# Two MLPs behind a delta attention: the second MLP's first weight blocks split during the first MLP, in single conversion steps, with raw blocks asked for later

## The chip, the core and the metric

The kernel runs on one core of a Trainium2 chip. The metric is device microseconds of one execution. Three timed runs of the kernel before gave 1169.36 us as the median (1157.91 to 1170.28).

## What is computed

```python
x = attention(q, k, v, beta)            # delta rule, 4 x 8 heads, 768 steps, head size 48
x = x.transpose(0, 2, 1, 3).reshape(3072, 384)

h = x @ w_in                            # first Mlp, d_ff = 2048
P = a[0] + a[1] * h + a[2] * h**2 + a[3] * h**3
Q = 1 + abs(b[0]) * abs(h) + abs(b[1]) * h**2
x = (P / (Q + 1e-6)) @ w_out

h = x @ w2_in                           # second Mlp, d_ff = 2048
out = (h * tanh(softplus(h))) @ w2_out  # Mish
```

All weights arrive in 64 bits. A conversion turns each pair of 32-bit words into one float32.

## The kernel before

The attention runs first, by a plan. Then come two Mlps in one software pipeline of 192 units, 96 for each: six groups g of 512 tokens, and in each group 16 blocks f of 128 hidden features. Unit i is one (g, f). In the loop over i each iteration emits, in the order of a string of `MLP_OPS`, steps of several units at once; `LAGS` says by how many units a step is behind.

Products are made of three passes: each float32 operand is split into a high part (rounded to the matmul's type) and a low part (the rest), and hi*hi, hi*lo and lo*hi are summed in PSUM. Unit i has an up-projection of nine matmuls (`up`, L827) into one of two PSUM banks h, and four units later a down-projection (`down`: L913 in the first Mlp, L946 in the second) into banks o. At the end of a group ACT evicts o through ev (L1035).

In the first Mlp the activation of a unit is spread over the engines: ACT takes q = |h| (L857); r = b1*q + b0 on ACT (L864, even units) or POOL (L860, odd units and units near an x split, by `m1.pool`); ACT s = a3*h + a2 (L866); POOL q = q*r (L870); ACT Ln (L877) and Exp (L879) for the quotient; VectorE the polynomial in two steps on h (L884, L886; behind L886 the bank h is free for the up-projection two units later) and three more (L893, L897, L902) that end in g. Two units later ACT makes the high part gh (L838) and POOL the low part (L842). In the order of ACT, Ln and Exp of unit i-1 come first in iteration i, then L857 of unit i, r, s, and gh of unit i-2. In the order of VectorE the three steps of unit i-1 come before the two of unit i.

The next group's x is split in units 11, 12 and 13 of each group: on ACT the high part (L807, ops "xa"), on VectorE the low one (L811, "xB").

The second Mlp's activation is two Mish instructions on ACT (L932 for the high part, L937 for g) and a subtraction for the low part (L842), on POOL where `m2.pool` has the unit and on VectorE elsewhere.

Weights. The first Mlp's 16 blocks are converted and split during the attention and stored in DRAM; two stay in SBUF, the other 14 are fetched at the start of the first Mlp (L730), all by SP's queue. The ring of tiles w holds 16 blocks. Block f of the second Mlp is needed from unit 96 + f.

The second Mlp's weights are converted by `Conv`, two sides (w_in, w_out) a block. A side is one raw load of 384 KB (L651), the magnitude (L663 on ACT, or L659 on VectorE once `free` is set) and three pulled steps on VectorE: "size" (L668, L672), "sign" (L678) and "low" (L684). When "low" of side j is emitted, the raw load of side j+3 is, too. What comes behind "low" is appended to a list of ACT work that op "f" empties at the end of the iteration. For the first eight blocks (`DIRECT`) that is a DMA from wm to DRAM, unsplit (L692); those blocks are fetched from iteration 94 on into wraw (L727), split by ACT (L733, op "wa") and by POOL (L737, op "wb") in iterations 95 to 102. For the other eight blocks, converted from unit 97 on at four steps an iteration, ACT copies the high part to w (L694) and POOL subtracts (L699).

In the first Mlp op "c" pulls three steps at once, in every fifth iteration: 12, 17, 22, ... 87. The first three raw loads are asked for by `conv.start()` ahead of the loop, before the first weight fetch.

Of the kernel before, what the change touches and what calls it, by code (L numbers as in the profile page):

```python
# [9 lines left out]
F32 = mybir.dt.float32  # L10
# [22 lines left out]
MLP_OPS = [  # L33
# [4 lines left out]
]  # L38
# [3 lines left out]
}  # L42
CONV_START, CONV_EARLY, CONV_RATE = 8, 16, 4

# [576 lines left out]
class Weights:  # L621
# [9 lines left out]

    def __init__(self, nc, w_in, w_out, sb, kept, direct, scratch):
        self.nc, self.sb, self.kept, self.direct, self.scratch = nc, sb, kept, direct, scratch
        self.w_in = w_in.rearrange("(k p) f -> p k f", p=128)
        self.w_out = w_out.rearrange("f (k c) -> f k c", c=128)
        self.raw = {}
        self.t = {}

    def tile(self, f):
        if f not in self.t:  # L640
            self.t[f] = self.sb.tile([128, 2, 2, 3, 128], F32R, "w")
        return self.t[f]

    def convert(self, f, side):
# [44 lines left out]
        def out():  # L689
            m = w["m"].bitcast(F32).rearrange("p (k c) -> p k c", k=3)  # L690
            if f not in self.direct:
                nc.sync.dma_start(out=self.scratch[f][:, side], in_=m)  # L692
                return
            nc.scalar.copy(out=self.tile(f)[:, 0, side], in_=m)  # L694
# [5 lines left out]

        return get, mag, size, sign, low, out, rest

    def plan(self, p, fs):

        slots = len(self.kept)
        for i, f in enumerate(fs):
            slot, late = f"w{i % slots}", LATE * i - AHEAD
            for side in range(2):
                n = 2 * i + side
                get, mag, size, sign, low, out, rest = self.convert(f, side)  # L710
                raw, m = f"w64{n % 2}", f"wm{n % 2}"
# [12 lines left out]

    def fetch(self, f):
        self.raw[f] = self.sb.tile([128, 2, 3, 128], F32, "wraw")
        self.nc.sync.dma_start(out=self.raw[f], in_=self.scratch[f])  # L727
# [4 lines left out]
    def hi(self, f):  # L732
        self.nc.scalar.copy(out=self.tile(f)[:, 0], in_=self.raw[f])  # L733

    def lo(self, f, engine="P"):
        t = self.tile(f)
        (self.nc.gpsimd if engine == "P" else self.nc.vector).tensor_tensor(  # L737
            out=t[:, 1], in0=self.raw.pop(f), in1=t[:, 0].bitcast(F32), op=ALU.subtract
        )


class Conv:


    def __init__(self, sides, direct):
        self.sides, self.direct = sides, direct
        self.act = []
        self.n = 0
        self.mags = 0
# [15 lines left out]
    def pull(self, n):  # L765
        for _ in range(n):
# [14 lines left out]
            if i == 2:  # L781
                self.act.append(side[5] if j < self.direct else lambda side=side: (side[5](), side[6]()))
                if j + 3 < len(self.sides):
                    self.sides[j + 3][0]()
# [172 lines left out]
def tile_delta_attention_two_mlps(  # L957
# [43 lines left out]

    wd = [[dram.tile([128] + [2] * (2 - n) + [3, 128], F32, name=f"w{n}_{f}") for f in range(NF)] for n in range(2)]
    w1 = Weights(nc, moe_w_in, moe_w_out, sb, range(FQ), range(NF), wd[0])
    w2 = Weights(nc, moe2_w_in, moe2_w_out, sb, (), range(DIRECT, NF), wd[1])
    def run(fns):
        for fn in fns:
            fn()

    conv = Conv([w2.convert(f, side) for f in range(NF) for side in range(2)], 2 * DIRECT)

# [66 lines left out]
    with ExitStack() as bctx:  # L1077
        sb2 = bctx.enter_context(tc.tile_pool(name="sb2", bufs=1, reuse_waits="tile"))
        ps2 = bctx.enter_context(tc.tile_pool(name="ps2", bufs=1, space=PSUM, reuse_waits="tile"))
        sb.add(sb2, w=16 - FQ, w64=1, wm=1, wraw=3, x=1, q=3, s=3, r=2, g=3, gh=5, ev=3)  # L1080
        ps.add(ps2, h=2, o=4, r=2)
        conv.start()
        fetch_w = {n: (w1.fetch_split, FQ + LOOK + n) for n in range(NF - FQ - LOOK)}
        split_w = {}
        for f in range(DIRECT):
            fetch_w[n1 - 2 + f] = (w2.fetch, f)
            split_w[n1 - 1 + f] = (w2, f)
        for f in range(LOOK):
# [10 lines left out]
        ups, downs = {}, {}  # L1099
        m1.pool = {i for i in range(n1) if i % 2 or i in split_w or any(starts(j) for j in range(i + 3, i + 6) if j < n2)}  # L1100
        m2.pool = [i for i in range(n1, n1 + NF) if i % 2]
        for i in range(n2 + max(LG.values())):
            kind = 3 if i >= n1 else 2 if i in split_w and i >= n1 - 1 else 0 if i in split_w else 1

# [6 lines left out]
            for op in LISTS[kind]:  # L1111
# [22 lines left out]
                elif op == "fx" and i + 8 < n2 and starts(i + 8):  # L1134
                    mlp(i + 8).fetch_x(units[i + 8][0])
                elif op == "wa" and i in split_w:
                    w, f = split_w[i]
                    w.hi(f)
                elif op in ("wb", "wB") and i in split_w:
                    w, f = split_w[i]  # L1140
                    w.lo(f, "P" if op == "wb" else "V")
# [41 lines left out]
```

## Time and profile before

| | us |
|---|---|
| median of three timed runs | 1169.36 |
| the profiled execution, its own time | 1159.04 |
| its span, first to last instruction | 1157.3 |
| TensorE busy | 1044.8 |
| VectorE busy | 722.6 |
| ACT busy | 612.6 |
| POOL busy | 532.6 |

The attention fills the span to about 320 us, the first Mlp goes on to about 735, the second to the end. Busy times are shares of engines that take turns; what limits a stage is read from what each engine waits for there. In a row of the trace, the number in brackets is the idle time of the engine in front of the instruction, and behind the arrow stands what ended it. "w" in a row is any of the weight tiles or raw tiles.

### The profile page before, as it was taken

How to read it: one execution, taken by the hardware profiler on the slowest of the kernel's cores; microseconds unless marked ns; L12 is line 12 of the kernel's file. 1: busy time of each engine (PE TensorE's matmuls, PEld its weight loads, DVE VectorE, ACT ScalarE, POOL GpSimd, SP SyncE). 2: the span in 40 equal slices, each digit the busy share in tenths (PEclk: the TensorE clock that was granted, in tenths of full speed). 3: DMA queues.
4: the chain of work that ended last, by engine and by line, in shares of the span. 5: the costliest groups of instructions: out<-in, count | busy, mean ns of one | idle time of the engine just before them, and what ended most of it. 6: DMA issues, size and time to landing. Idle time of an engine off the chain costs nothing.

```text
span 1157.3 us, 24281 instructions
## 1 busy us (share of the span) xinstructions
PE 1044.8 (90%) x9980; PEld 903.6 (78%) x9980; DVE 722.6 (62%) x1214; ACT 612.6 (53%) x1093; POOL 532.6 (46%) x607
## 2 busy tenths in 40 slices
PE   5649869688879898999999999999999999999998
PEld 4538868577858777877778778678999999999997
DVE  5877575995658999899898999786121121212110
ACT  4415445334468787888888888754333223333322
POOL 3178787477347676777677767774000000000000
PEclk9858879789889999999999999999999999999999
DMA  7427676226692020120212022152100001010000
GB/s 140 84 64 179 171 209 146 77 58 194 189 364 105 21 96 21 48 69 21 76 41 76 21 69 89 36 197 68 55 1 30 26 1 55 1 55 1 28 1 28
DMA packets 122415, 92.90 MB, mean 80 GB/s; under 512 B 79936, under 2 KB 106688, under 8 KB 122304
## 3 DMA queue, kind: packets, MB, share of 16 engines
q1 hardware_dynamic: 122048, 91.25, 26.9%
q8 instruction: 78, 1.28, 0.4%
q14 instruction: 33, 0.27, 0.1%
q0 software_dynamic: 256, 0.10, 0.1%
HBM read 63.02 MB, written 28.31 MB: 79 GB/s over the span
## 4 chain that ended last, share of the span: by engine, by line
PE 46%; POOL 17%; DVE 14%; ACT 12%; issue 9%; DMA 2%; SPq 0%; POOLq 0%; DVEq 0%; ACTq 0%
PE h L827 17%; PE o L946 15%; POOL q L870 8%; ACT r L877 3%; POOL r L860 3%; POOL gh L842 3%; PE y_ps L562 3%; ACT q L857 2%; PE c_ps L524 2%; ACT r L879 2%; PE c_ps L507 2%; PE s_all L547 2%; PE o L913 2%; DVE tmp L447 1%; PE t_ps L348 1%
## 5 line engine op out<-in xcount | busy, mean ns | idle before, releaser
L827 PE MATMUL h<-x,w 128*128 128x512 f32 x1728 | 435.8, 397 | 23.2 <-DVE s L886 12.1
L827 PEld LDWEIGHTS h<-x,w 128*128 128x128 f32 x1728 | 323.8, 190 | 97.6 <-DVE s L886 26.7
L842 DVE TENSOR_TENSOR gh<-g,gh 128x512 fp32r<-128x512 f32 x88 | 63.8, 725 | 285.3 <-ACT g L937 285.3
L946 PE MATMUL o<-w,gh 128*128 128x384 f32 x1152 | 217.4, 337 | 2.0 <-ACT ev L1035 2.0
L913 PE MATMUL o<-gh,w 128*128 128x512 f32 x864 | 213.7, 391 | 0.5 <-ACT ev L1035 0.4
L946 PEld LDWEIGHTS o<-w,gh 128*128 128x128 f32 x1152 | 204.5, 188 | 10.8 <-ACT ev L1035 2.7
L913 PEld LDWEIGHTS o<-gh,w 128*128 128x128 f32 x864 | 162.8, 189 | 36.2 <-ACT ev L1035 2.2
L932 ACT ACTIVATE gh<-h 128x512 fp32r<-128x512 f32 x96 | 57.6, 600 | 213.0 <-PE h L827 213.0
L870 POOL TENSOR_TENSOR q<-q,r 128x512 f32<-128x512 f32 x96 | 127.9, 1332 | 80.4 <-ACT r L864 75.9
L842 POOL TENSOR_TENSOR gh<-g,gh 128x512 fp32r<-128x512 f32 x104 | 136.8, 1315 | 8.9 <-ACT g L937 4.9
L877 ACT ACTIVATE r<-q,cst 128x512 f32<-128x512 f32 x96 | 66.4, 692 | 61.0 <-POOL q L870 60.8
L893 DVE SCALAR_TENSOR_TENSOR q<-q,r 128x512 f32<-128x512 f32 x96 | 65.6, 683 | 27.4 <-ACT r L879 27.0
L699 POOL TENSOR_TENSOR w<-wm,w 128x384 fp32r<-128x384 f32 x48 | 48.4, 1009 | 72.5 <-ACT w L694 71.9
L866 ACT ACTIVATE s<-h,ab 128x512 f32<-128x512 f32 x96 | 74.4, 775 | 0.0
L886 DVE SCALAR_TENSOR_TENSOR s<-s,ab,h 128x512 f32<-128x512 f32 x96 | 71.8, 748 | 3.4
L897 DVE SCALAR_TENSOR_TENSOR r<-s,ab,r 128x512 f32<-128x512 f32 x96 | 71.8, 748 | 0.0
L884 DVE TENSOR_TENSOR s<-s,h 128x512 f32<-128x512 f32 x96 | 65.4, 681 | 10.1 <-ACT s L866 10.1
L902 DVE SCALAR_TENSOR_TENSOR g<-q,r 128x512 f32<-128x512 f32 x96 | 65.9, 687 | 3.3
L453 POOL TENSOR_TENSOR xs<-xs,tmp 128x30 f32<-128x30 f32 (+14 forms) x120 | 62.2, 519 | 9.4
L857 ACT ACTIVATE q<-h 128x512 f32<-128x512 f32 x96 | 57.1, 595 | 12.6 <-PE h L827 12.6
L860 POOL TENSOR_SCALAR r<-q,ab 128x512 f32<-128x512 f32 x54 | 43.4, 804 | 43.1 <-ACT q L857 43.1
L447 POOL TENSOR_TENSOR tmp<-xs 128x30 f32<-128x30 f32 (+14 forms) x120 | 58.5, 487 | 7.0
(123 smaller groups left out, 1322.9 us busy)
## 6 DMA issues: line engine op xcount, KB each, us to landing
w<-w SPq DMA_DIRECT2D x28, 768.0 KB, 7.4
w<-in_moe_w_in_dram SPq DMA_DIRECT2D x32, 384.0 KB, 3.7
w<-in_moe_w_out_dram SPq DMA_DIRECT2D x32, 384.0 KB, 3.6
xraw<-x SPq DMA_DIRECT2D x36, 256.0 KB, 4.0
kn<-in_k_dram SPq DMA_DIRECT2D x48, 96.0 KB, 3.5
qn<-in_q_dram SPq DMA_DIRECT2D x48, 96.0 KB, 3.3
v<-in_v_dram SPq DMA_DIRECT2D x48, 96.0 KB, 3.4
x<-yst SPq DMA_DIRECT2D x24, 192.0 KB, 4.1
```

The costliest lines, as they stand in the source:

```text
L447: eng.tensor_tensor(out=tv, in0=ls[:, j, j + 1:HC].unsqueeze(1).to_broadcast([128, j, n]), in1=xs[:, 0:j, j:j + 1].to_broadcast([128, j, n ...
L827: self.nc.tensor.matmul(out=self.st[i]["h"], lhsT=self.w.t[f][:, a, 0, k], rhs=self.x[g][:, b, k], start=(n == 0), stop=(n == 8),)
L842: (nc.gpsimd if engine == "P" else nc.vector).tensor_tensor(out=s["gh"][:, 1], in0=s["g"], in1=s["gh"][:, 0].bitcast(F32), op=ALU.subtract)
L857: nc.scalar.activation(out=s["q"], in_=s["h"], func=ACTF.Abs)
L860: nc.gpsimd.tensor_scalar(out=s["r"], in0=s["q"], scalar1=k["b1"], scalar2=k["b0"], op0=ALU.mult, op1=ALU.add)
L866: nc.scalar.activation(out=s["s"], in_=s["h"], func=ACTF.Identity, scale=k["a3"], bias=k["a2"])
L870: nc.gpsimd.tensor_tensor(out=s["q"], in0=s["q"], in1=s["r"], op=ALU.mult)
L877: nc.scalar.activation(out=s["r"], in_=s["q"], func=ACTF.Ln, bias=k["c"])
L886: nc.vector.scalar_tensor_tensor(out=s["s"], in0=s["s"], scalar=k["a1"], in1=s["h"], op0=ALU.add, op1=ALU.mult)
L897: nc.vector.scalar_tensor_tensor(out=s["r"], in0=s["s"], scalar=k["a0"], in1=s["r"], op0=ALU.add, op1=ALU.mult)
L913: self.nc.tensor.matmul(out=self.acc[g][d], lhsT=self.w.t[f][:, a, 1, d], rhs=self.st[i]["gh"][:, b], start=(first and n == 0), stop=(last ...
L946: self.nc.tensor.matmul(out=self.acc[g][t][:, 0:384], lhsT=self.st[i]["gh"][:, a, t * 128:(t + 1) * 128], rhs=self.w.t[f][:, b, 1].rearran ...
```

## The change

- The first eight blocks of the second Mlp are treated as the others: ACT copies the high part (into a tile wt, of which there is one), POOL subtracts, and after the second side a DMA stores the split block (768 KB). They are fetched split, straight into w, in iterations 86 to 93. The fetch into wraw, L733 and L737 with the ops "wa" and "wb" are gone, and two of the four strings of `MLP_OPS` with them.
- In the first Mlp, op "c" works only in iterations of `calm`: 6 to 87 without those that split x (11, 12 and 13 of each group). The 48 steps of the 16 sides are spread over these 67 iterations, at most one in each. "Low" falls into iterations 10, 17, 21, 25, 32, 37, 41, 48, 52, 56, 64, 68, 72, 79, 83 and 87.
- `conv.start()` moves into iteration 3, behind eight weight fetches.
- `m2.pool` takes all of the second Mlp's first 16 units, no longer the odd ones alone.

```diff
-CONV_START, CONV_EARLY, CONV_RATE = 8, 16, 4
+CONV_START, CONV_RATE = 6, 4
...
+        self.tag = {f: "wt" for f in passing}
...
-            self.t[f] = self.sb.tile([128, 2, 2, 3, 128], F32R, "w")
+            self.t[f] = self.sb.tile([128, 2, 2, 3, 128], F32R, self.tag.get(f, "w"))
...
-            if f not in self.direct:
-                nc.sync.dma_start(out=self.scratch[f][:, side], in_=m)
-                return
             nc.scalar.copy(out=self.tile(f)[:, 0, side], in_=m)
...
+        def done():
+            if side and f in self.tag:
+                self.store(f)
...
     def store(self, f):
+        self.tag.pop(f, None)
...
-                self.act.append(side[5] if j < self.direct else lambda side=side: (side[5](), side[6]()))
+                self.act.append(lambda side=side: [f() for f in side[5:]])
...
-        conv.start()
...
-            fetch_w[n1 - 2 + f] = (w2.fetch, f)
-            split_w[n1 - 1 + f] = (w2, f)
+            fetch_w[n1 - NF + 6 + f] = (w2.fetch_split, f)
+        calm = [i for i in range(CONV_START, n1 - 8) if not any(starts(i + 5 - k) for k in range(3))]
...
-        m2.pool = [i for i in range(n1, n1 + NF) if i % 2]
+        m2.pool = range(n1, n1 + NF)
...
+            if i == CONV_START - 3:
+                conv.start()
...
-                elif op == "c" and i >= CONV_START:
-                    conv.pull(max(0, 3 * min(CONV_EARLY, CONV_EARLY * (i + 1 - CONV_START) // (n1 - 8 - CONV_START)) - conv.n))
+                elif op == "c" and i in calm:
+                    conv.pull(6 * DIRECT * (calm.index(i) + 1) // len(calm) - conv.n)
```

How the instructions stand on three engines. Line numbers of the change are lower: L682 is L684 of before, L689 is L694, L825 is L838, L864 is L877, L866 is L879, L873 is L886, L880 is L893.

SP's queue at the start of the first Mlp, behind the last stores of the attention. Before, three raw loads and then the first fetches:

```order
L651 DMA w_4760<-in_moe_w_in_dram 128x3x128
L651 DMA w_4762<-in_moe_w_out_dram 128x384
L651 DMA w_4764<-in_moe_w_in_dram 128x3x128
L730 DMA w<-w_2_82 128x1536
L730 DMA w<-w_3_83 128x1536
```

And with the change:

```order
L613 DMA x_5_65<-yst_155 48x8x128 x4
L726 DMA w<-w_2_82 128x1536
L726 DMA w<-w_3_83 128x1536
L726 DMA w<-w_4_84 128x1536
L726 DMA w<-w_5_85 128x1536
L726 DMA w<-w_6_86 128x1536
L726 DMA w<-w_7_87 128x1536
L726 DMA w<-w_8_88 128x1536
L726 DMA w<-w_9_89 128x1536
L649 DMA w_4850<-in_moe_w_in_dram 128x3x128
```

Eight fetches now stand ahead of the first raw load.

VectorE in iteration 12 of the kernel before, where a side is converted in one piece behind the low part of x (L811):

```order
L884 TENSOR_TENSOR s<-s,h 128x512
L886 SCALAR_TENSOR_TENSOR s<-s,ab,h 128x512
L811 TENSOR_TENSOR x<-xraw,x 128x512
L668 TENSOR_SCALAR wm<-wm 128x384
L672 TENSOR_SCALAR wm<-wm 128x384
L678 SCALAR_TENSOR_TENSOR wm<-w_4760,wm 128x384
L684 SCALAR_TENSOR_TENSOR wm<-w_4760,wm 128x384
L893 SCALAR_TENSOR_TENSOR q<-q,r 128x512
```

With the change, iteration 10 has "low" alone on VectorE:

```order
L871 TENSOR_TENSOR s<-s,h 128x512
L873 SCALAR_TENSOR_TENSOR s<-s,ab,h 128x512
L682 SCALAR_TENSOR_TENSOR wm<-w_4850,wm 128x384
L880 SCALAR_TENSOR_TENSOR q<-q,r 128x512
L884 SCALAR_TENSOR_TENSOR r<-s,ab,r 128x512
```

"Size" and "sign" of that side stand in iterations 7 and 8, between L873 and L880 as "low" does here.

ACT at the end of iteration 10 and the start of iteration 11, with the change (the kernel before has L838 and then L877 here, with nothing between them):

```order
L853 ACTIVATE s<-h,ab 128x512
L825 CAST gh<-g 128x512
L689 CAST wt<-wm 128x384
L864 ACTIVATE r<-q,cst 128x512
L866 ACTIVATE r<-r 128x512
L844 ACTIVATE q<-h 128x512
```

The copy to wt, which reads what "low" wrote, stands between gh of unit 8 and Ln (L864) of unit 10. There are 16 such places.

## Rows read from the trace of the kernel before

**Rows 1.** The page: the chain that ended last, shares of the span by line.

```profile
PE h L827 17%; PE o L946 15%; POOL q L870 8%; ACT r L877 3%; POOL r L860 3%; POOL gh L842 3%; PE y_ps L562 3%; ACT q L857 2%; PE c_ps L524 2%; ACT r L879 2%; PE c_ps L507 2%; PE s_all L547 2%; PE o L913 2%; DVE tmp L447 1%; PE t_ps L348 1%
```

**Rows 2.** Windows: stretch, us, each engine's busy us, granted clock, DMA share, GB/s.

```profile
330.00:340.00 10.00, 8.97 (x26) 6.90 (x27) 4.68 (x7) 5.29 (x10) 3.16 (x3) 0.68 1.02 420
...
338.20:735.30 397.10, 385.03 (x1656) 311.00 (x1657) 364.45 (x544) 329.50 (x553) 281.97 (x238) 0.99 0.19 64
...
735.30:763.00 27.70, 22.57 (x94) 16.75 (x94) 21.64 (x37) 17.14 (x30) 22.75 (x16) 1.00 0.36 117
```

**Rows 3.** Timeline of units 9 and 10: start, us, engine, line, operation.

```profile
363.38 0.59 ACT L857 ACTIVATE q<-h 128x512 f32<-128x512 f32 x1
...
366.34 0.69 ACT L877 ACTIVATE r<-q,cst 128x512 f32<-128x512 f32 x1 [1.19 <-POOL q L870]
...
367.56 0.59 ACT L857 ACTIVATE q<-h 128x512 f32<-128x512 f32 x1
...
370.34 1.29 POOL L842 TENSOR_TENSOR gh<-g,gh 128x512 fp32r<-128x512 f32 x1
370.41 0.69 ACT L877 ACTIVATE r<-q,cst 128x512 f32<-128x512 f32 x1 [0.23 <-POOL q L870]
370.46 0.75 DVE L886 SCALAR_TENSOR_TENSOR s<-s,ab,h 128x512 f32<-128x512 f32 x1
...
371.63 0.59 ACT L857 ACTIVATE q<-h 128x512 f32<-128x512 f32 x1
```

**Rows 4.** ACT from 338.20 to 735.30 by line (busy, mean ns, idle before), and its timeline.

```profile
L877 ACT ACTIVATE r<-q,cst 128x512 f32<-128x512 f32 x92 | 63.6, 692 | 56.0 <-POOL q L870 55.9
...
L857 ACT ACTIVATE q<-h 128x512 f32<-128x512 f32 x93 | 55.3, 595 | 6.3 <-PE h L827 6.3
...
342.78 0.59 ACT L857 ACTIVATE q<-h 128x512 f32<-128x512 f32 x1
...
407.79 0.59 ACT L857 ACTIVATE q<-h 128x512 f32<-128x512 f32 x1
...
412.44 0.61 ACT L857 ACTIVATE q<-h 128x512 f32<-128x512 f32 x1
...
735.10 0.60 ACT L857 ACTIVATE q<-h 128x512 f32<-128x512 f32 x1
```

**Rows 5.** VectorE by line in that stretch, then the timeline around unit 15.

```profile
L684 DVE SCALAR_TENSOR_TENSOR wm<-w,wm 128x384 int32<-128x384 int32 x16 | 15.1, 942 | 0.6
...
382.23 1.54 DVE L684 SCALAR_TENSOR_TENSOR wm<-w,wm 128x384 int32<-128x384 int32 x1
...
387.19 3.91 PE L827 MATMUL h<-x,w 128*128 128x512 f32 x9 [3.01 <-DVE s L886]
```

**Rows 6.** Timeline of the first Mlp's start; the last row: DMA issues there.

```profile
320.01 0.67 SPq L651 DMA_DIRECT2D w<-in_moe_w_in_dram  x1
...
330.32 7.17 PE L827 MATMUL h<-x,w 128*128 128x512 f32 x18 [6.41 <-DMA w<-w]
...
334.54 0.60 ACT L857 ACTIVATE q<-h 128x512 f32<-128x512 f32 x1 [4.42 <-PE h L827]
...
w<-in_moe_w_in_dram SPq DMA_DIRECT2D x2, 384.0 KB, 5.5
```

**Rows 7.** The hand-over, 735.3 to 763, by line.

```profile
L827 PE MATMUL h<-x,w 128*128 128x512 f32 x45 | 12.3, 406 | 3.1 <-ACT w L733 1.2 <-ACT g L937 1.1 <-POOL w L737 0.8
L737 POOL TENSOR_TENSOR w<-wraw,w 128x768 fp32r<-128x768 f32 x6 | 11.5, 1916 | 3.2 <-ACT w L733 3.2
...
L699 POOL TENSOR_TENSOR w<-wm,w 128x384 fp32r<-128x384 f32 x4 | 4.2, 1039 | 2.5 <-ACT w L694 2.5
...
L946 PE MATMUL o<-w,gh 128*128 128x384 f32 x12 | 2.8, 355 | 2.0 <-ACT ev L1035 2.0
...
L684 DVE SCALAR_TENSOR_TENSOR wm<-w,r 128x384 int32<-128x384 int32 x5 | 2.8, 551 | 0.1
L694 ACT CAST w<-wm 128x384 fp32r<-128x384 f32 x5 | 2.6, 521 | 7.9 <-DVE wm L684 7.9
```

More of the change, by code (lines that the diff above doesn't have):

```diff
@@ L33 @@
 MLP_OPS = [
[1 row of a table removed]
     "fx fw y0 1e 1f y1 u0 u1 u2 1a 1b 1c 1i 1j 1k 1d 1g 1h y2 d0 d1 d2 d3 xa 1L 1m xB c f",
[2 rows of a table removed]
+    "fx fw y0 1e 1f y1 2a 2b u0 u1 u2 1i 1j 1k y2 d0 v0 2M d1 v1 d2 v2 d3 v3 xa 1L 1m xB c f",
 ]
@@ L630, with __init__ @@
     word = None
-    def __init__(self, nc, w_in, w_out, sb, kept, direct, scratch):
-        self.nc, self.sb, self.kept, self.direct, self.scratch = nc, sb, kept, direct, scratch
+    def __init__(self, nc, w_in, w_out, sb, kept, passing, scratch):
+        self.nc, self.sb, self.kept, self.scratch = nc, sb, kept, scratch
+        self.tag = {f: "wt" for f in passing}
         self.w_in = w_in.rearrange("(k p) f -> p k f", p=128)
         self.w_out = w_out.rearrange("f (k c) -> f k c", c=128)
-        self.raw = {}
         self.t = {}
@@ L699, in rest @@
             nc.gpsimd.tensor_tensor(out=t[:, 1, side], in0=m, in1=t[:, 0, side].bitcast(F32), op=ALU.subtract)
-        return get, mag, size, sign, low, out, rest
+        def done():
+            if side and f in self.tag:
+                self.store(f)
+        return get, mag, size, sign, low, out, rest, done
     def plan(self, p, fs):
@@ L709, in plan @@
                 n = 2 * i + side
-                get, mag, size, sign, low, out, rest = self.convert(f, side)
+                get, mag, size, sign, low, out, rest, _ = self.convert(f, side)
                 raw, m = f"w64{n % 2}", f"wm{n % 2}"
@@ L722, in store, with __init__ @@
     def store(self, f):
+        self.tag.pop(f, None)
         self.nc.sync.dma_start(out=self.scratch[f], in_=self.t.pop(f).bitcast(F32))
-    def fetch(self, f):
-        self.raw[f] = self.sb.tile([128, 2, 3, 128], F32, "wraw")
-        self.nc.sync.dma_start(out=self.raw[f], in_=self.scratch[f])
     def fetch_split(self, f):
         self.nc.sync.dma_start(out=self.tile(f).bitcast(F32), in_=self.scratch[f])
[L732 to L739, printed above, removed]
 class Conv:
-    def __init__(self, sides, direct):
-        self.sides, self.direct = sides, direct
+    def __init__(self, sides):
+        self.sides = sides
         self.act = []
@@ L1000, in tile_delta_attention_two_mlps @@
     n2 = len(units)
-    wd = [[dram.tile([128] + [2] * (2 - n) + [3, 128], F32, name=f"w{n}_{f}") for f in range(NF)] for n in range(2)]
-    w1 = Weights(nc, moe_w_in, moe_w_out, sb, range(FQ), range(NF), wd[0])
-    w2 = Weights(nc, moe2_w_in, moe2_w_out, sb, (), range(DIRECT, NF), wd[1])
+    wd = [[dram.tile([128, 2, 2, 3, 128], F32, name=f"w{n}_{f}") for f in range(NF)] for n in range(2)]
+    w1 = Weights(nc, moe_w_in, moe_w_out, sb, range(FQ), (), wd[0])
+    w2 = Weights(nc, moe2_w_in, moe2_w_out, sb, (), range(DIRECT), wd[1])
     def run(fns):
@@ L1007, in run @@
             fn()
-    conv = Conv([w2.convert(f, side) for f in range(NF) for side in range(2)], 2 * DIRECT)
+    conv = Conv([w2.convert(f, side) for f in range(NF) for side in range(2)])
     m1 = Mlp1(nc, w1, sb, ps, x1, consts)
@@ L1079, in tile_delta_attention_two_mlps @@
         ps2 = bctx.enter_context(tc.tile_pool(name="ps2", bufs=1, space=PSUM, reuse_waits="tile"))
-        sb.add(sb2, w=16 - FQ, w64=1, wm=1, wraw=3, x=1, q=3, s=3, r=2, g=3, gh=5, ev=3)
+        sb.add(sb2, w=16 - FQ, wt=1, w64=1, wm=1, x=1, q=3, s=3, r=2, g=3, gh=5, ev=3)
         ps.add(ps2, h=2, o=4, r=2)
-        conv.start()
         fetch_w = {n: (w1.fetch_split, FQ + LOOK + n) for n in range(NF - FQ - LOOK)}
-        split_w = {}
         for f in range(DIRECT):
-            fetch_w[n1 - 2 + f] = (w2.fetch, f)
-            split_w[n1 - 1 + f] = (w2, f)
+            fetch_w[n1 - NF + 6 + f] = (w2.fetch_split, f)
+        calm = [i for i in range(CONV_START, n1 - 8) if not any(starts(i + 5 - k) for k in range(3))]
         for f in range(LOOK):
@@ L1099, in tile_delta_attention_two_mlps @@
         ups, downs = {}, {}
-        m1.pool = {i for i in range(n1) if i % 2 or i in split_w or any(starts(j) for j in range(i + 3, i + 6) if j < n2)}
-        m2.pool = [i for i in range(n1, n1 + NF) if i % 2]
+        m1.pool = {i for i in range(n1) if i % 2 or any(starts(j) for j in range(i + 3, i + 6) if j < n2)}
+        m2.pool = range(n1, n1 + NF)
         for i in range(n2 + max(LG.values())):
-            kind = 3 if i >= n1 else 2 if i in split_w and i >= n1 - 1 else 0 if i in split_w else 1
+            kind = int(i >= n1)
+            if i == CONV_START - 3:
+                conv.start()
             def at_x(f):
@@ L1135, in tile_delta_attention_two_mlps @@
                     mlp(i + 8).fetch_x(units[i + 8][0])
[L1136 to L1141, printed above, removed]
                 elif op == "xa":
```

3 rows, old and new, of the table MLP_OPS are left out of this document.

## The prediction

> **What bounds the kernel now.** I read the page first, then the stages one by one. In the chain that ended last the largest lines are TensorE's, but L870, L877, L860, L857 and L879, the activation of the first Mlp on POOL and ACT, hold 18% of it [rows 1]. So TensorE's share does not say what limits the first Mlp. The windows split the run: the steady part of the first Mlp takes 397.1 us with TensorE busy 385.0, the hand-over to the second Mlp 27.7 us with TensorE busy 22.6 [rows 2]. Of the second Mlp behind it the change touches nothing but the queues of its first units. So there are three places to look at: the start of the first Mlp, its steady part, and the hand-over.
>
> The steady part is read from an odd and an even unit [rows 3]. ACT takes |h| (L857) at 363.38, 367.56 and 371.63: 4.18 us for an odd unit (POOL makes r), 4.07 for an even one (ACT makes r). Between two of them lies a closed loop: L857, r, POOL's product L870, ACT's Ln (L877, at +2.96 and +2.85 after L857), Exp (L879), and at once the next L857. Over the stretch ACT waited 55.9 us for POOL in front of L877, and only 6.3 us for TensorE in front of L857, in 92 units [rows 4]. So the loop through ACT and POOL paces the first Mlp, at 4.125 us on the mean, and TensorE is ready a little earlier. What is put into this loop is not won back, since the loop has no slack of its own.
>
> From L857 of unit 4 (342.78) to that of unit 95 (735.10) are 91 periods in 392.3 us [rows 4]. 45 odd ones at 4.18 and 46 even ones at 4.07 make 375.3, so 17.0 us are excess. Evictions are part of it: a period with two of them, from 407.79 to 412.44, is 4.65 instead of 4.18 [rows 4], so three cost about 0.7, and five groups 3.5 us, which stay. The other 13.5 I put down to the conversion: four VectorE steps in one unit, on top of an x split, hold VectorE (one L684 takes 1.54 us), L886 comes late, and TensorE waits 3.01 us for the h bank [rows 5].
>
> **The change, part by part.**
>
> *Single steps away from x splits.* 16 sides now come as 48 single steps. "Size" and "sign" stand behind L886, where VectorE waits for the next Exp: L886 of the even unit ends at 371.21, Exp just before 371.7 [rows 3]. About half a microsecond is free there, a step of one or two instructions runs over by as much again at most, and it is off the loop. I credit the whole 13.5 us, which flatters the change.
>
> *Conversion with a split.* For the eight first blocks the result of step "low" (L684) used to leave by DMA from wm. Now ACT copies it to wt, and the copy stands in ACT's order between L838 of a unit and Ln of the same unit. It has to wait for "low", and "low" stands behind L886 on VectorE. In the hand-over of the kernel before, this wait is seen: five copies L694 of 0.521 us with 7.9 us of ACT idle in front of them, for DVE wm L684 [rows 7]. The cost, with T the start of L857: L886 starts at T+2.90 and ends at T+3.65 [rows 3]; "low" takes 0.942 us on the mean of the first Mlp [rows 5] and ends near T+4.57; the copy's 0.52 let Ln start near T+5.0, since neighbours on ACT overlap by 0.1. Ln stood at T+2.85 or T+2.96. That is 2.1 us in the loop for each of 16 sides, 33.6 us. Bounds: "low" at 0.55 us, as in the hand-over [rows 7], gives 1.7 us, 27.2 in all; at 1.54 [rows 5] 2.7 us, 43. I take 2.1, since 0.942 is measured in this same stretch. Queued behind the copy are Ln, Exp and the next L857; VectorE's L893 waits for Exp, and TensorE's h bank for L886.
>
> The 16 POOL subtractions (1.04 us, as L699 [rows 7]) start when the copy ends, T+5.1, and end at T+6.1, while ACT is at Ln and Exp; POOL's next job waits for the next L857. Hidden; without that cover 1.0 us each. Eight stores and eight fetches of 768 KB replace sixteen and eight smaller ones, where the DMA engines are at 0.19 [rows 2]; a fetch stands ten units ahead of its use, so it is hidden too.
>
> *Raw blocks later.* Three raw loads of 384 KB stood in SP's queue ahead of the first weight fetch, the first of them issued at 320.01. TensorE waited 6.41 us for the block of unit 2, then took 7.17 us for eighteen matmuls, and L857 of unit 2 came at 334.54 after 4.42 us of waiting for TensorE [rows 6]: ACT was done with unit 1 at 330.1. Now the fetch goes out near 320.0. A raw load of this stretch landed 5.5 us after issue [rows 6], so the block is there near 325.5, and its nine matmuls are done before 330.1 even at half clock. Gain 4.4 us, ACT's whole wait; 0 if the block came as late as before. The raw loads now stand behind eight fetches: 7.5 MB at the 420 GB/s of 330 to 340 [rows 2] are 18 us, so they are there near 340. ACT first needs them in unit 6, two periods behind 342.78 - 4.4, near 347. Hidden, or conversion starts a few units late.
>
> *Hand-over.* Five units take 27.7 us; at 4.125 they would take 20.6, so 7.1 are excess. Gone are ACT's copy L733 and POOL's subtraction L737 (1.92 us each), for which TensorE waited 1.2 and 0.8 us in front of L827, and which delayed the gates it also waited for (L937, 1.1). What stays are 2.0 us for the evictions, which stand behind the conversion's copies on ACT [rows 7]. The gain lies between 5.1 and 7.1; I take 6.1. The subtractions of the gate that move from VectorE to POOL use the time that L737 leaves.
>
> *Sum.* Start -4.4; steady part +33.6 - 13.5 = +20.1; hand-over -6.1: **+9.6 us**. On the profiled execution's own 1159.04 us this is 1168.6. That execution lies 10.3 below the median of the three runs, 1169.36; on the median the sum is **1179.0 us**, 0.8% more.
>
> **The rivals.**
>
> *The wait is absorbed, and the kernel gets faster.* If TensorE and not the loop paced the first Mlp, two h banks would hide 2.1 us, and only the gains remain: -4.4 - 13.5 - 6.1 = -24.0, 1145.4 us. For it: TensorE is busy 385.0 of 397.1 us [rows 2]. Against it: ACT waited for TensorE only 6.3 us in 92 units [rows 4]. It decides from the point where L857 waits for TensorE by 2 us in each unit with a "low". The Trainium skill, "Perfetto Trace Analysis", section "Optimizing Scalar/DVE Operations", says that breaking up instructions may let work finish sooner where ScalarE or VectorE is not saturated but causes bubbles on other engines; the single steps are such a case. The bubble of 3.01 us agrees [rows 5], but the rule does not speak of a copy that joins another engine's order.
>
> *"Low" is short once it stands alone.* 27.2 instead of 33.6 gives +3.2, 1172.6. For it: 0.55 us in the hand-over [rows 7]. Against it: POOL's L842 runs from T+2.78 to T+4.07 [rows 3], over the start of "low", and the 0.942 comes from units with that same L842. The Trainium skill, "SBUF — State Buffer", section "Who interferes with whom", says that a VectorE instruction with two SBUF inputs contends with a GpSimd one that reads SBUF, and that the one that comes later is blocked for the whole of the other. By it "low" cannot begin before T+4.07 and the sum is the forecast's +9.6 or a little more; without it, it is this rival's +3.2. The 0.942 against 0.55 us agrees with it.
>
> *The hand-over gains nothing*, because the conversion's copies still hold ACT and the evictions stand behind them: +9.6 + 6.1 = +15.7, 1185.1. For it: the 7.9 us of ACT. Against it: 3.1 of TensorE's 5.1 us of waits there name L733, L737 and L937 [rows 7].
>
> *The clock falls in each gap.* A gap of 3.01 us was followed by nine matmuls in 3.91 us [rows 5]; half of that, 1.95, is what half clock costs. Sixteen gaps near 2 us with that each make +31, +40.8 in all, 1210.2. Against it: at the start of a period TensorE has been done for up to 2 us, which hides it.
>
> **How the numbers follow.** Forecast 0.53 (own range 1174 to 1186), short "low" 0.15, no gain at the hand-over 0.13, absorbed wait 0.13, clock 0.06. The range 1160 to 1190 leaves out the last two, and reaches down to times near the profiled execution's (1159.04 + 3.2 = 1162.2). Less than 1% can't be told from no change here: the bounds are 1157.7 and 1181.1. Faster: the absorbed wait, 0.13. Slower: clock 0.06, most of "no gain" 0.12 and the upper third of the forecast 0.17, together 0.35. The same: 0.52.
>
> **What would show it.** In the changed profile: ACT idle in front of 16 copies to wt, for DVE wm, and periods of L857 near 6.2 us in those units, 4.07 and 4.18 elsewhere; no TensorE wait over 1 us behind x splits; L857 of unit 2 near 330; a hand-over of 21 to 23 us. Wrong would be: periods near 4.1 in units with a "low", or well under 1 us of idle ACT in front of the copy.

## The result, and the profile after

| | before | changed |
|---|---|---|
| median of 17 runs each, us | 1161.11 | 1174.36 |
| lowest and highest | 1156.79, 1171.83 | 1165.67, 1182.96 |
| span of the profiled execution | 1157.3 | 1168.3 |

The changed kernel takes 1.0105 times as long, with a 95% interval of 1.0082 to 1.0128: 13.2 us more on the medians. The interval leaves out 1, so the changed kernel is the slower one, by 1.05%: just past the 1% up to which the prediction calls two times the same. The forecast was +9.6 us on the profiled execution, and 1179.0 us (1160 to 1190) in all. Runs of one and the same kernel scatter by some 15 us, and in the ten profiles unit 0 starts anywhere between 318.35 and 332.93 us (last section). So the parts are compared below by stretches of the traces behind unit 0. The 91 periods repeat within half a microsecond in kernels that have them alike (413.52 twice; 382.61, 382.65 and 383.08). The start and the hand-over repeat less well, which is said where they are read.

Line numbers are smaller in the changed kernel. The loop of [rows 3] is now L844 (|h|), r, L857 (POOL's product), L864 (Ln), L866 (Exp); the second half of s is L873, "low" L682, the conversion's copy L689, its subtraction L694, the evictions L1022.

The page has the same three lines in the chain that ended last as in [rows 1]: TensorE's two and POOL's product.

```profile
PE h L814 18%; PE o L933 17%; POOL q L857 6%; ACT r L864 3%; ACT r L866 3%; POOL r L847 2%; PE c_ps L522 2%; PE y_ps L560 2%; ACT q L844 2%; DVE q L880 2%; DVE g L889 2%; DVE r L884 2%; DVE s L871 2%; DVE s L873 2%; DVE tmp L445 2%
```

Windows of the changed kernel: L844 of unit 4 to L844 of unit 95, then the hand-over, start of unit 96 to start of unit 101 (columns as in [rows 2]).

```profile
335.94:749.46 413.52, 384.64 (x1639) 303.14 (x1638) 360.41 (x537) 331.39 (x563) 287.74 (x250) 1.00 0.23 82
749.43:773.00 23.57, 21.53 (x94) 17.69 (x94) 21.86 (x36) 14.11 (x27) 15.42 (x15) 0.98 0.28 93
```

The 91 periods took 392.3 us before [rows 4] and take 413.5 now; the hand-over took 27.7 [rows 2] and takes 23.6. One of the sixteen long periods, unit 10, in the timeline (start, us, engine, line, operation, idle before and what ended it):

```profile
360.70 0.59 ACT L844 ACTIVATE q<-h 128x512 f32<-128x512 f32 x1
...
363.48 1.31 POOL L829 TENSOR_TENSOR gh<-g,gh 128x512 fp32r<-128x512 f32 x1
363.61 0.75 DVE L873 SCALAR_TENSOR_TENSOR s<-s,ab,h 128x512 f32<-128x512 f32 x1
364.28 0.93 DVE L682 SCALAR_TENSOR_TENSOR wm<-w,wm 128x384 int32<-128x384 int32 x1
...
365.24 0.51 ACT L689 CAST wt<-wm 128x384 fp32r<-128x384 f32 x1 [1.92 <-DVE wm L682]
...
365.66 0.69 ACT L864 ACTIVATE r<-q,cst 128x512 f32<-128x512 f32 x1
365.83 1.02 POOL L694 TENSOR_TENSOR wt<-wm,wt 128x384 fp32r<-128x384 f32 x1 [1.04 <-ACT wt L689]
...
366.87 0.59 ACT L844 ACTIVATE q<-h 128x512 f32<-128x512 f32 x1
```

The copy starts at T+4.54, Ln at T+4.96, and the next L844 at T+6.17, where an even unit has 4.07 [rows 3]. So the Ln of this unit is 2.1 us late, and with it all that is behind it. ACT's lines from 336 to 749.5 show the sixteen together (busy, mean ns, idle before): the copy brings 37.9 us of idle time, while Ln's own wait for POOL falls from 55.9 us [rows 4] to 40.0, since POOL has finished in the meantime.

```profile
L864 ACT ACTIVATE r<-q,cst 128x512 f32<-128x512 f32 x91 | 62.8, 690 | 40.0 <-POOL q L857 40.0
...
L689 ACT CAST wt<-wm 128x384 fp32r<-128x384 f32 x16 | 8.2, 513 | 37.9 <-DVE wm L682 37.9
```

At the start, L844 of units 1 and 2 stand 4.63 us apart, not the 8.59 of the kernel before (325.95 to 334.54), with 0.44 us of ACT waiting for TensorE in place of 4.42 [rows 6]:

```profile
323.07 0.59 ACT L844 ACTIVATE q<-h 128x512 f32<-128x512 f32 x1
...
327.70 0.60 ACT L844 ACTIVATE q<-h 128x512 f32<-128x512 f32 x1 [0.44 <-PE h L814]
```

Over all profiles this distance is 4.08 to 5.38 us with the raw loads later (eight kernels) and 8.59 and 9.43 with them in front (two). So the gain is some 3 to 5 us, and 4.0 in this pair.

At the hand-over TensorE's waits for w and g of [rows 7] are gone from the lines between 749.43 and 773.00; the one for the evictions is not. It is 2.0 us as before, and the mean of L933 is 405 ns where it was 355 [rows 7]:

```profile
L814 PE MATMUL h<-x,w 128*128 128x512 f32 x45 | 11.1, 390 | 0.0
L900 PE MATMUL o<-gh,w 128*128 128x512 f32 x37 | 9.2, 389 | 0.0
L933 PE MATMUL o<-w,gh 128*128 128x384 f32 x12 | 3.3, 405 | 2.0 <-ACT ev L1022 2.0
```

The parts are -4.0 us at the start, +21.2 in the 91 periods and -4.2 at the hand-over, +13.0 in all, against the medians' +13.2, which the interval leaves open by 2.7 us either way. The profiled spans differ by only 11.0. In the changed kernel's profiled execution unit 0 came 2.9 us earlier (319.03 against 321.90), which lies within the scatter of its start.

### The profile page after: what moved, and what is told of

Read it like the earlier page. It is cut to its first block, busy times and chain, and to the rows that moved or that the text cites. A ratio compares the mean times of both kernels' runs of the same rounds, so it can differ in the third digit from the quotient of the medians.

```text
span 1168.3 us, 24287 instructions
## 1 busy us (share of the span) xinstructions
PE 1047.8 (90%) x9980; PEld 899.8 (77%) x9980; DVE 719.2 (62%) x1206; ACT 612.7 (52%) x1101; POOL 536.9 (46%) x623
## 4 chain that ended last, share of the span: by engine, by line
PE 46%; DVE 19%; ACT 14%; POOL 10%; issue 6%; DMA 2%; SPq 2%; POOLq 0%; DVEq 0%; ACTq 0%
PE h L814 18%; PE o L933 17%; POOL q L857 6%; ACT r L864 3%; ACT r L866 3%; POOL r L847 2%; PE c_ps L522 2%; PE y_ps L560 2%; ACT q L844 2%; DVE q L880 2%; DVE g L889 2%; DVE r L884 2%; DVE s L871 2%; DVE s L873 2%; DVE tmp L445 2%
## 5 line engine op out<-in xcount | busy, mean ns | idle before, releaser
L814 PE MATMUL h<-x,w 128*128 128x512 f32 x1728 | 435.1, 396 | 25.9 <-DVE s L873 21.3
L814 PEld LDWEIGHTS h<-x,w 128*128 128x128 f32 x1728 | 320.7, 189 | 105.5 <-DVE s L873 38.3
L829 DVE TENSOR_TENSOR gh<-g,gh 128x512 fp32r<-128x512 f32 x80 | 55.4, 693 | 281.0 <-ACT g L924 281.0
L933 PE MATMUL o<-w,gh 128*128 128x384 f32 x1152 | 217.9, 337 | 2.0 <-ACT ev L1022 2.0
L933 PEld LDWEIGHTS o<-w,gh 128*128 128x128 f32 x1152 | 204.8, 188 | 10.8 <-ACT ev L1022 2.7
L857 POOL TENSOR_TENSOR q<-q,r 128x512 f32<-128x512 f32 x96 | 124.5, 1297 | 74.3 <-ACT r L851 68.3
L829 POOL TENSOR_TENSOR gh<-g,gh 128x512 fp32r<-128x512 f32 x112 | 145.2, 1297 | 17.1 <-ACT g L924 14.6
L880 DVE SCALAR_TENSOR_TENSOR q<-q,r 128x512 f32<-128x512 f32 x96 | 65.5, 682 | 47.9 <-ACT r L866 47.9
L864 ACT ACTIVATE r<-q,cst 128x512 f32<-128x512 f32 x96 | 66.3, 690 | 44.9 <-POOL q L857 44.9
L694 POOL TENSOR_TENSOR w<-wm,w 128x384 fp32r<-128x384 f32 x48 | 48.6, 1012 | 66.8 <-ACT w L689 66.6
L873 DVE SCALAR_TENSOR_TENSOR s<-s,ab,h 128x512 f32<-128x512 f32 x96 | 71.8, 748 | 3.4
L847 POOL TENSOR_SCALAR r<-q,ab 128x512 f32<-128x512 f32 x54 | 41.9, 776 | 42.4 <-ACT q L844 42.4
L825 ACT CAST gh<-g 128x512 fp32r<-128x512 f32 x96 | 59.8, 622 | 0.0
```

The lines of the kernel that those rows point to most:

```text
L814: self.nc.tensor.matmul(out=self.st[i]["h"], lhsT=self.w.t[f][:, a, 0, k], rhs=self.x[g][:, b, k], start=(n == 0), stop=(n == 8),)
L829: (nc.gpsimd if engine == "P" else nc.vector).tensor_tensor(out=s["gh"][:, 1], in0=s["g"], in1=s["gh"][:, 0].bitcast(F32), op=ALU.subtract)
L857: nc.gpsimd.tensor_tensor(out=s["q"], in0=s["q"], in1=s["r"], op=ALU.mult)
L864: nc.scalar.activation(out=s["r"], in_=s["q"], func=ACTF.Ln, bias=k["c"])
L873: nc.vector.scalar_tensor_tensor(out=s["s"], in0=s["s"], scalar=k["a1"], in1=s["h"], op0=ALU.add, op1=ALU.mult)
L880: nc.vector.scalar_tensor_tensor(out=s["q"], in0=s["q"], scalar=1.0 + 1e-6, in1=s["r"], op0=ALU.add, op1=ALU.mult)
```

## The experiments

My theory was the forecast's: a wait put into the closed loop of ACT and POOL lengthens it by its whole length. The main rival was that the lengthening comes from the work itself, or from TensorE, so that the wait alone is nothing.

### The copy one unit later

```diff
-                self.act.append(lambda side=side: [f() for f in side[5:]])
+                (self.held if j < 2 * DIRECT else self.act).append(lambda side=side: [f() for f in side[5:]])
...
                 elif op == "f":
                     conv.flush()
+                    conv.act, conv.held = conv.held, []
```

> The changed kernel with one thing undone: the copy of a finished conversion side to wt (with the subtraction and the store behind it) is put into ACT's order one unit later, so that the step 'low' that it needs lies some 4 us back. Everything else is the same. My theory (the copy's wait for 'low' is held inside the closed loop of ACT and POOL, 2.1 us in each of 16 units): the 16 long periods of 6.2 us vanish, the copy's own 0.52 us lies in the 0.6 us per unit that ACT waits for POOL in front of Ln, the 91 periods from unit 4 to unit 95 fall from 413.5 us to 376 to 384, and the kernel becomes 30 to 37 us faster than the changed one: a profiled span of 1131 to 1139, a ratio of 0.975 to 0.985 against the kernel before. Rival (the lengthening has another cause, such as TensorE's own pace or the copy's and the subtraction's work, of which nothing is taken away here): 413.5 falls by less than 8 us and the kernel stays at or above the one before.

Measured: 0.982 times the kernel before (0.9777 to 0.9862). The 91 periods take 382.61 us (339.14 to 721.75), 30.9 less than in the changed kernel. The subtraction and the store behind each copy move with it. The same sixteen copies now start without a wait, and Ln waits for POOL again, as it did before the change (ACT, 339.2 to 721.7):

```profile
L865 ACT ACTIVATE r<-q,cst 128x512 f32<-128x512 f32 x91 | 62.9, 691 | 47.6 <-POOL q L858 47.6
...
L689 ACT CAST wt<-wm 128x384 fp32r<-128x384 f32 x16 | 8.4, 522 | 0.0
```

No work was taken away; only its place in the order, and with it the wait, changed. The rival "work or TensorE" falls. What the copy costs where it doesn't wait is seen in one unit: between L826 and Ln there was room for it, and Ln still waits 0.26 us for POOL.

```profile
369.62 0.65 ACT L826 CAST gh<-g 128x512 fp32r<-128x512 f32 x1
370.14 0.54 ACT L689 CAST wt<-wm 128x384 fp32r<-128x384 f32 x1
370.93 0.69 ACT L865 ACTIVATE r<-q,cst 128x512 f32<-128x512 f32 x1 [0.26 <-POOL q L858]
```

### "Low" twice

```diff
+            if f in self.tag:
+                nc.vector.scalar_tensor_tensor(
+                    out=w["m"], in0=word(0), scalar=29, in1=w["x"],
+                    op0=ALU.logical_shift_right, op1=ALU.bitwise_or,
+                )
```

> The changed kernel with the step 'low' of each of the 16 sides done twice in a row by VectorE (the second gives the same bits). My theory: ACT's copy stands behind both, so each of 16 periods grows from about 6.2 us by the length of the second 'low', 0.55 us if it then lies behind POOL's subtraction, 0.88 if it is as long as the first: the 91 periods from 413.5 to 422 to 428 us, the kernel 9 to 14 us slower than the changed one. The second 'low' also tells why the first takes 0.88 us: if POOL's subtraction of the same time lengthens it, the second is 0.55. Rival (the wait is absorbed by the second h bank, the lengthening comes from elsewhere): no change, 413.5 plus or minus 2.

Measured: 1.0178 times the kernel before (1.0113 to 1.0242); the 91 periods take 422.53 us, 9.0 more than in the changed kernel, and a period with "low" 6.75 in place of 6.17. So 0.558 us more on VectorE, which is off the loop, sixteen times, come out whole in the stretch (8.9 of 9.0 us), through ACT's copy (here L694). VectorE's two lines:

```profile
L682 DVE SCALAR_TENSOR_TENSOR wm<-w,wm 128x384 int32<-128x384 int32 x16 | 14.9, 932 | 0.0
...
L687 DVE SCALAR_TENSOR_TENSOR wm<-w,wm 128x384 int32<-128x384 int32 x16 | 8.9, 558 | 0.6
```

The first "low" takes 932 ns on the mean, the same instruction right behind it 558. Each of the sixteen first ones begins while POOL makes the low part of gh (L829 in the changed kernel); none of the second ones does.

### Raw blocks later, alone

The kernel before, with one edit:

```diff
-        conv.start()
...
+            if i == CONV_START - 5:
+                conv.start()
```

> The kernel before with one part of the change alone: the three raw loads are issued in iteration 3 of the loop instead of ahead of it, behind the weight fetches. My theory: the first weight fetch goes out at once, the block of unit 2 lands earlier, and L857 of unit 2 comes some 4 us earlier (unit 1 to unit 2 in 4.1 to 4.6 us instead of 8.6), a ratio of 0.996 to 0.997. Rival: the fetch is bound by the memory's rate and the gain is zero, or what is won here is lost again as a later wait for the raw blocks.

Measured: 0.996 times the kernel before (0.9926 to 0.9994). L857 of units 1 and 2 stand at 331.01 and 335.11, 4.10 us apart in place of 8.59, and ACT no longer waits for TensorE in front of the second. The 91 periods are 392.99 us, as before (392.32): what is won at the start is not lost to a later wait for the raw blocks.

### Single steps, alone

The kernel before, with one edit (calm is the list of the changed kernel, made by the same line with this kernel's CONV_START, 8):

```diff
-                elif op == "c" and i >= CONV_START:
-                    conv.pull(max(0, 3 * min(CONV_EARLY, CONV_EARLY * (i + 1 - CONV_START) // (n1 - 8 - CONV_START)) - conv.n))
+                elif op == "c" and i in calm:
+                    conv.pull(3 * CONV_EARLY * (calm.index(i) + 1) // len(calm) - conv.n)
```

> The kernel before with one part of the change alone: the conversion in the first Mlp goes in single steps away from x splits; its results still leave by DMA from wm and are fetched and split as before. My theory: the excess of 17.0 us over the 91 periods from unit 4 to unit 95 falls to about 3.5 to 6, the stretch from 392.3 to 379 to 382 us, no TensorE wait of over 1 us behind x splits, and the kernel is 10 to 13 us faster than before, a ratio of 0.988 to 0.991. Rival (the bursts' waits were not what made the excess): the stretch stays at 390 or more and the ratio at 0.997 to 1.0.

Measured: 0.9867 times the kernel before (0.9821 to 0.9914). The 91 periods take 380.33 us in place of 392.32, the hand-over 27.8, as before:

```profile
354.04:734.37 380.33, 373.93 (x1638) 305.37 (x1636) 358.50 (x538) 325.16 (x548) 271.73 (x234) 1.00 0.19 62
734.52:762.29 27.77, 22.65 (x94) 16.83 (x95) 21.91 (x38) 17.20 (x30) 22.77 (x16) 1.00 0.37 118
```

and TensorE's L827 has 0.1 us of idle time in front of it in all 91 periods, where a single x split cost 3.01 in [rows 5]:

```profile
L827 PE MATMUL h<-x,w 128*128 128x512 f32 x819 | 201.5, 390 | 0.1
```

So 12.0 us of the 17.0 were the bursts of conversion steps. This one edit alone stands at 0.9867 where the whole change stands at 1.0105.

### No conversion step where the evictions are due

The changed kernel, with the steps of iteration n1+3 left out (each later step comes one unit later):

```diff
+                elif op == "c" and i == n1 + LAG - 1:
+                    pass
                 elif op == "c" and i > n1:
```

> The changed kernel with one unit of the second Mlp left without conversion steps: none in iteration n1+3, so that ACT's three evictions (L1022) of the last group of the first Mlp no longer stand behind two copies that wait for 'low'. The later steps each come one unit later. My theory (the hand-over gained 4 instead of 6 us because the evictions still stand behind those copies, and TensorE waits 1.4 us for a bank and then runs a dozen matmuls at half clock): the gap of 1.4 us in the first down part of the second Mlp goes, the clock stays up, the hand-over (start of unit 96 to start of unit 101) falls from 23.6 to 20.5 to 21.5 us, and the kernel is 2 to 3 us faster than the changed one, a ratio of 1.007 to 1.009 against the kernel before. Rival (the wait moves to a converted block that now comes too late, or the banks wait for something else): the hand-over stays at 23 or more, or a new TensorE wait of 2 us appears within the next ten units.

What it takes away is seen in the changed kernel, ACT and then TensorE around the evictions:

```profile
766.50 0.51 ACT L689 CAST w<-wm 128x384 fp32r<-128x384 f32 x1 [2.08 <-DVE wm L682]
768.88 0.51 ACT L689 CAST w<-wm 128x384 fp32r<-128x384 f32 x1 [1.87 <-DVE wm L682]
769.29 1.07 ACT L1022 COPY ev<-o 128x512 f32<-128x512 f32 x2
...
```

```profile
767.84 0.68 PE L933 MATMUL o<-w,gh 128*128 128x384 f32 x3
769.93 1.31 PE L933 MATMUL o<-w,gh 128*128 128x384 f32 x6 [1.40 <-ACT ev L1022]
771.88 1.33 PE L933 MATMUL o<-w,gh 128*128 128x384 f32 x3 [0.64 <-ACT ev L1022]
```

Two copies wait 2.08 and 1.87 us for "low", the evictions stand behind them in ACT's order, and TensorE waits for the banks that they free. Behind these gaps the granted clock was 0.50 from 771.91 to 775.32. Measured: the hand-over falls to 20.48 us, in all of which TensorE is busy:

```profile
748.55:769.03 20.48, 20.48 (x94) 17.31 (x94) 19.00 (x29) 13.56 (x26) 14.53 (x13) 1.00 0.27 91
```

Up to the start of unit 110 the gain is 4.1 us (58.16 in place of 62.29), the clock's part included; no new wait appears. The kernel with "low" twice shows how large that part is: it has the same steps and nearly the same waits here (1.37 and 0.62 us), but kept its clock. These are its matmuls on o in the hand-over, and a window behind the second wait as long as the one at 0.50 above:

```profile
L938 PE MATMUL o<-w,gh 128*128 128x384 f32 x12 | 2.8, 355 | 2.0 <-ACT ev L1027 2.0
785.68:789.09 3.41, 3.41 (x17) 3.02 (x18) 3.27 (x7) 2.31 (x6) 3.41 (x4) 1.00 0.85 282
```

Its hand-over takes 23.02 us, and up to unit 110 it takes 60.70. So about 2.5 of the 4.1 us are the evictions' wait and 1.6 are the clock, which fell behind these waits in the changed kernel and in the one with the copy one unit later (0.51), and not in this one.

The ratio to the kernel before is 1.0093 (1.0062 to 1.0125), against 1.0105 for the changed kernel. That is just outside the 1.007 to 1.009 that I expected, and 4 us are near what the runs can tell, so the verdict rests on the trace.

### Both edits, twice

> The two edits together on the changed kernel: the copy to wt one unit later, and no conversion step in iteration n1+3. My theory: the gains add, since they lie in stretches apart: the 91 periods take 382 to 383 us (as with the copy alone), the hand-over 20.5 to 21.5, and the kernel is 2 to 3 us faster than with the copy alone: a profiled span of 1136 to 1140, a ratio of 0.978 to 0.981 against the kernel before, faster than both kernels. Rival: the evictions come late for another reason once the steady part is shorter, and the ratio stays at 0.982 or above.

> The kernel with the copy one unit later and no conversion step in iteration n1+3, a second time, beside the kernel with the copy on VectorE. My theory: as the first time, 382 to 383 us for the 91 periods, 20.5 for the hand-over; over both measurements a ratio of 0.976 to 0.986 against the kernel before, and no difference over 0.5% to the copy on VectorE. Rival: a ratio of 0.987 or above again, so that the hand-over's 3 us do not add to the gain of the copy put off alone (0.982).

Measured: 0.9873 (0.9823 to 0.9923) the first time, 0.9835 (0.9784 to 0.9885) the second; the 91 periods 382.65 and 383.08 us, the hand-over 20.49 and 20.50. In the stretches the gains add. In the times they don't show: the first ratio missed the 0.978 to 0.981 that I expected and lies where its rival had it. The mean of the two, 0.985, is within the 0.976 to 0.986 expected for both, but six runs each can't tell it from the copy put off alone (0.982) or the single steps alone (0.9867). The lowest time is 1135.50 us. Both intervals lie below 1, so the kernel with both edits is faster than both kernels, by some 1.5% against the one before.

### The copy on VectorE

The kernel without steps in iteration n1+3, with the copy to wt made by VectorE behind "low":

```diff
-            nc.scalar.copy(out=self.tile(f)[:, 0, side], in_=m)
+            if f in self.tag:
+                nc.vector.tensor_copy(out=self.tile(f)[:, 0, side], in_=m)
+            else:
+                nc.scalar.copy(out=self.tile(f)[:, 0, side], in_=m)
```

> As the kernel without conversion steps in iteration n1+3, but the copy to wt is made by VectorE, right behind 'low' in VectorE's own order, and no longer by ACT; nothing is deferred. The work is the same, only its engine differs. My theory (what costs is the place of the wait, inside the closed loop of ACT and POOL, not the wait or the work as such): ACT waits for nothing new, VectorE carries 0.4 to 0.55 us more in 16 units, where it has about 0.57 us free per unit and may run over by some tenths, and the 91 periods fall from 413.5 to 380 to 388 us, as with the copy put off by a unit (382.6); a ratio of 0.978 to 0.986 against the kernel before. Rival (the conversion's chain from 'low' through the copy to POOL's subtraction is long wherever it lies, or VectorE becomes the bound): periods of 5 us and more in the 16 units, 395 us or more in all, a ratio of 0.992 or above.

Measured: 0.9892 (0.9842 to 0.9942); the 91 periods take 390.92 us, between what I and the rival expected. (The kernel with both edits, measured beside it, had 0.9835. That is 0.6% less, over the 0.5% that I expected, but the two intervals overlap.) ACT's wait is gone, but I had overlooked who comes next. The timeline shows it:

```profile
370.03 0.59 ACT L847 ACTIVATE q<-h 128x512 f32<-128x512 f32 x1
...
370.48 0.36 DVE L690 CAST wt<-wm 128x384 fp32r<-128x384 f32 x1
...
370.92 1.02 POOL L697 TENSOR_TENSOR wt<-wm,wt 128x384 fp32r<-128x384 f32 x1 [0.89 <-DVE wt L690]
...
371.92 0.78 POOL L850 TENSOR_SCALAR r<-q,ab 128x512 f32<-128x512 f32 x1
...
374.11 0.69 ACT L867 ACTIVATE r<-q,cst 128x512 f32<-128x512 f32 x1 [1.80 <-POOL q L860]
...
375.33 0.59 ACT L847 ACTIVATE q<-h 128x512 f32<-128x512 f32 x1
```

Here L847 is |h| of an odd unit. Its r (L850) could start near 370.8, as POOL's r stands 0.77 behind |h| elsewhere, but POOL is at the conversion's subtraction until 371.94. The period is 5.30 in place of 4.18: the 1.02 us of the subtraction are now in the loop, on its other engine. Eight odd units have 5.30 to 5.56 us; seven even ones, where ACT makes r, have 4.41 to 4.44, and unit 84 has 4.24. It is the same mechanism as with the copy, one engine further on. In the changed kernel the subtraction fell into the time in which the loop stood still for the copy: it ended at 366.85, and the next |h| began at 366.87.

## Why the prediction was right

| step | forecast, us | measured | from |
|---|---|---|---|
| start | -4.4 | -4.0 | 8.59 to 4.63; alone 8.59 to 4.10, -4.5; scatter about 1 us |
| bursts gone | -13.5 | -12.0 | 392.32 to 380.33, alone |
| copy waits for "low" | +33.6 | +33.2 | 380.33 to 413.52 |
| hand-over | -6.1 | -4.2 | 27.72 to 23.57 |
| sum | +9.6 | +13.0 | medians +13.2 |

**The copy.** Periods of 6.2 us were named, and 6.15 to 6.26 came in thirteen of the sixteen units; three with an eviction's copies on ACT as well had 6.58 and 7.19. The step T+2.90 to T+3.65 (L886), then "low" to T+4.57, Ln near T+5.0, came out as T+2.91, T+4.51 and T+4.96. The rival of the absorbed wait falls by its own mark: L844 had no wait for TensorE at all in this stretch. Of the 33.2 us, 30.9 went when the copy came one unit later.

**The length of "low".** The rival of a short "low" falls too: 936 ns on the mean in the changed kernel. That this meets the 942 ns of the forecast so closely was luck, though. I said that the 942 came from units with the same POOL instruction on gh, and that was a misreading: of the sixteen "low" of the kernel before, six took 0.56 us, seven 1.01 to 1.02 and three 1.53 to 1.54, and only one of the last three began while L842 ran. The seven began while POOL made r (L860) and ended about 0.41 us behind it; the six began with no POOL instruction under way:

```profile
404.82 0.56 DVE L684 SCALAR_TENSOR_TENSOR wm<-w,wm 128x384 int32<-128x384 int32 x1
...
425.81 0.99 POOL L860 TENSOR_SCALAR r<-q,ab 128x512 f32<-128x512 f32 x1 [0.86 <-ACT q L857]
426.19 1.02 DVE L684 SCALAR_TENSOR_TENSOR wm<-w,wm 128x384 int32<-128x384 int32 x1
```

What holds is the other argument of the prediction, that "low" has to wait for L842 to end at T+4.07; in the changed kernel all sixteen meet that instruction (now L829). All sixteen end about 0.41 us behind POOL's L829 which they meet; where L829 began late, "low" is long:

```profile
414.96 0.64 DVE L682 SCALAR_TENSOR_TENSOR wm<-w,wm 128x384 int32<-128x384 int32 x1
...
413.89 1.30 POOL L829 TENSOR_TENSOR gh<-g,gh 128x512 fp32r<-128x512 f32 x1
```

```profile
556.50 1.37 DVE L682 SCALAR_TENSOR_TENSOR wm<-w,wm 128x384 int32<-128x384 int32 x1
...
556.15 1.30 POOL L829 TENSOR_TENSOR gh<-g,gh 128x512 fp32r<-128x512 f32 x1 [0.36 <-ACT gh L825]
```

415.60 is 0.41 behind 415.19, and 557.87 is 0.42 behind 557.45. In the second Mlp, where the scratch x of "low" lies in PSUM and only one of its inputs in SBUF, it takes 0.55 us while L829 runs:

```profile
757.62 0.55 DVE L682 SCALAR_TENSOR_TENSOR wm<-w,r 128x384 int32<-128x384 int32 x1
...
756.73 2.54 POOL L829 TENSOR_TENSOR gh<-g,gh 128x512 fp32r<-128x512 f32 x2 [1.11 <-ACT g L924]
```

The Trainium skill, "SBUF — State Buffer", section "Who interferes with whom", says that a VectorE instruction with two SBUF inputs contends with a GpSimd instruction that reads SBUF, and that the port pair which they share is an exclusive lock. These rows agree with it, the case in PSUM included.

**The bursts.** The 13.5 us were called flattering, and 12.0 were there. The Trainium skill, "Perfetto Trace Analysis", section "Optimizing Scalar/DVE Operations", says that breaking up instructions may help where an engine is not saturated but makes bubbles on others; the single steps alone agree with it (TensorE's wait in front of L827 is 0.1 us), though here a burst of instructions was broken up and not one instruction.

**The hand-over** is the step that was mis-sized; at 23.57 us it also lies outside the 21 to 23 that I had named as a sign. The rival of no gain falls, with 4.2 us gained. I let the evictions' 2.0 us of waiting stay and credited 6.1 of the 7.1 us of excess. The wait did stay at 2.0, but the excess left is 3.1 (23.57 less 20.48), not 1.0. With the 2.0 us of waiting come 0.8 us of slower matmuls, twelve times 405 less 337 ns, the mean where nothing waits (no step at the evictions):

```profile
L933 PE MATMUL o<-w,gh 128*128 128x384 f32 x12 | 2.3, 337 | 0.0
```

In the kernel before, and in the one with "low" twice, these matmuls took 355 ns on the mean: there the clock stayed up behind the same wait. So the clock has about 0.6 of the 0.8 us. 7.1 less the 2.0 that stay was my lower bound, 5.1; I took 6.1 as if half of that wait would go as well, and priced no clock behind it. Even with the clock up the gain is 4.7 (27.72 less 23.02), under that bound. Which part of the change gained how much here, the fetch of split blocks or the subtractions moved to POOL, no run tells apart.

**The clock.** The rival of a fall in each gap didn't come. Behind the long periods TensorE has fourteen gaps of 0.82 to 1.76 us in front of L814, and the granted clock stays at 1.00, the upper of the two levels of 1.2 and 2.4 GHz, in them and behind them. The first window here lies around the first of these gaps:

```profile
369.06:371.06 2.00, 0.47 (x2) 0.43 (x3) 1.96 (x4) 1.31 (x4) 1.96 (x2) 1.00 0.00 0
700.23:703.64 3.41, 3.22 (x7) 2.12 (x8) 1.99 (x3) 3.35 (x7) 0.86 (x2) 0.50 0.80 268
```

In the 91 periods it fell once (the second window), behind a gap of 2.66 us where an eviction stood behind a copy (unit 83):

```profile
700.35 3.36 PE L900 MATMUL o<-gh,w 128*128 128x512 f32 x6 [2.66 <-ACT ev L1022]
```

**The time itself.** 1179.0 was 1169.36, the median of three runs, and 9.6. The median of seventeen runs of the kernel before is 1161.11, so the base was 8 us too high and the sum 3.5 too low. These two errors point opposite ways and partly cancel; from the right base the forecast would have been 1170.7, 3.7 us below the measured time.

## What to carry to other kernels

Look for the closed loop between engines that paces a stage, and price what is put into the order of any of its engines by how late its input is, not by how long it takes: here 0.5 us of copying cost 2.1 us each time, and about 0.14 (382.61 less 380.33, over sixteen, with its subtraction) when it came one unit later. Moving the step to another engine moved a third of the price along to the next engine of the loop (390.92 less 380.33 is 10.6 us, in place of 33.2); putting it off until its input was long there removed nearly all of it. And a change of several parts is worth taking apart: one part of this one was worth -12 us, and another cost 33.

## What was not expected of the hardware

The same kernel with both edits was profiled twice, with spans of 1134.8 and 1147.1 us. L845 of unit 0 came at 321.02 and 332.93, so 11.9 of the 12.3 us lie ahead of the first Mlp, where the same 6,246 matmuls were busy for 242.0 and 253.9 us at a granted clock of 0.83 and 0.79:

```profile
0.00:321.02 321.02, 242.01 (x6246) 218.69 (x6247) 229.89 (x470) 132.25 (x263) 196.32 (x329) 0.83 0.55 138
```

```profile
0.00:332.93 332.93, 253.94 (x6246) 230.73 (x6247) 230.85 (x470) 132.43 (x263) 196.72 (x329) 0.79 0.53 133
```

So in this kernel a difference of a few microseconds in a later stage is drowned by what the clock does in the attention, and has to be read from the stage's own stretch. Why the clock is granted differently there stays open.
